# Two buffers of x and of the outputs, a new order of steps, and products of q on GpSimd in a linear-attention and rational-feed-forward kernel

## The chip, the cores and the metric

The kernel runs on one core of a Trainium2 chip. The time is that of one execution on the device in microseconds; lower is better. The core has five engines that run their own instruction lists in order and wait for each other by semaphores: TensorE (PE; PEld is its loading of weights), VectorE (DVE), ScalarE (ACT), GpSimd (POOL) and SyncE (SP), which here only issues DMAs. Sixteen DMA engines serve the queues of SP, GpSimd and ACT.

## The reference

```python
# attention: q, k, v, f_logit are (4, 8, 768, 48)
f = 1.0 / (1.0 + np.exp(-f_logit))
for t in range(S):
    state = f[:, :, t, :, None] * state + np.einsum('bhd,bhe->bhde', k[:, :, t], v[:, :, t])
    y[:, :, t] = np.einsum('bhd,bhde->bhe', q[:, :, t], state)
# x: y as (3072, 384); w_in (384, 2048), w_out (2048, 384)
h = x @ w_in
h2 = h * h
h3 = h2 * h
P = a[0] + a[1] * h + a[2] * h2 + a[3] * h3
Q = 1.0 + np.abs(b[0]) * np.abs(h) + np.abs(b[1]) * h2
g = P / (Q + 1e-06)
out = g @ w_out
```

## The kernel before, in words

The work is cut into 12 units of 256 positions. Unit n belongs to batch n % 4 and to the third n // 4 of its sequence, so unit n needs the state that unit n-4 left. A unit has two parts of 128 positions, j = 0 and 1.

Nothing is scheduled by a planner at build time. A long text, `ORDER`, lists every step by hand-readable name, and the kernel emits the steps in that order; each engine runs its own steps in the order of the text. `@i` names the PSUM slot (four of them, of two banks each). `!m` marks a step, and `^m` makes another begin only behind the marked one. The text calls the second pair a tie: products on GpSimd begin behind a chosen VectorE step, `wi` (loads of w_in) behind the landing of unit 1's k (`^w`).

The steps of a unit, with the engine and the line of the helper:

- `ld n f|k|q|v` loads (L205): f, k, q on SP's queue, v on GpSimd's. f, k, q and v have three buffers each. A load in two pieces is written `ld 0 k 0 2; ld 0 k 2 4`.
- `ef`, `ls` (ACT, L279, L284): exp and log of the gate, as log f; `cs` (PE, L294, L299): its running sum by triangular matrices.
- `A n x` (ACT, L307): exp of the running sum, for q (x = 0) and k (x = 1). There is one buffer for each x, so the next unit's `A` waits until the product has read it. `ae` (ACT, L438) does the same for a whole part.
- `xa n x` (L312): the product of q or k with `A`, on VectorE, or on GpSimd where a `p` stands behind it.
- `T`, `Te`: transposes of both products on PE (L326), and their copy out of PSUM (L333), on ACT where an `s` stands behind it and else on VectorE.
- `sc`, `mk` (PE L347, DVE L355): scores and their mask. `vm` (L362) copies pieces of v. `yi`, `yb` (PE, L367): y from the state and from the scores. `ic`, `si`, `st` (PE L413, L422, DVE L442): the next state.
- `ye` (ACT L430 or DVE L432): y scaled into x in bf16.
- `h` (PE, L451): a group of four blocks of x times w_in, twelve matmuls; `hy` (ACT, L468) copies them out; 16 blocks to a unit.
- `sq`, `ab`, `p1`, `p2`, `pm`, `gm` (DVE, L472 to L534): squares, absolute values, the numerator and the quotient.
- `zd` and `ta` (L498, L526): additions made by adding DMAs from GpSimd's queue; `zv` and `tv` (DVE, L494, L530) are the same additions on VectorE, and `u` with `ln` (PE L484, ACT L489) is a third way for the first one.
- `lz`, `ex` (ACT, L502, L507): the reciprocal of Q as the exp of minus its log.
- `o` (PE, L543): g times w_out; `oe` (L550): its copy; `so` (L559): two stores on SP's queue.

Before, x has four buffers, and the outputs one, `osb`; the last three units write their outputs into the buffers of f, which are free by then.

## Time and profile before

| | |
|---|---|
| median of 3 runs | 223.18 us (222.46 to 224.02) |
| the profiled execution's own time | 221.77 us |
| its span, first to last instruction | 220.1 us |
| ACT busy | 196.8 us (89%) |
| DVE busy | 196.3 us (89%) |
| PE busy | 193.1 us (88%) |
| POOL busy | 82.3 us (37%) |
| data moved | 44.23 MB, mean 201 GB/s |
| granted TensorE clock | 0.987 |

A busy share is an average over the whole span. Which engine sets the end has to be read stage by stage, from the windows and the chain of waits. Instructions of ACT and DVE overlap a little with the next of the same engine, so a duration is somewhat longer than the distance from one start to the next. Each row of a timeline gives start and duration in us, engine, line, operation, output and input tiles, and in brackets the idle time before it and what ended it.

### The profile page before, as it was taken

Reading aid. Unit: us, or ns where it says so; the run is one execution under the profiler, and the core shown is the slowest. Engines: PE = TensorE matmul, PEld = TensorE weight load, DVE = VectorE, ACT = ScalarE, POOL = GpSimd, SP = SyncE. Lnnn points to the kernel's source line nnn. Section 1 sums busy time; section 2 is a strip of 40 time slices with the busy share of each in tenths; the row PEclk is TensorE's granted clock in tenths of the full one; section 3 lists DMA queues with packets and bytes.
Section 4 is the critical chain, followed back from the end, with each engine's and each line's share of the span. In section 5 each row is a group of like instructions: output and inputs, shape, how many; then the busy total and the mean of one; then the engine's idle time right before and its main releaser. Section 6 shows DMA issues by size and latency. Waiting matters only on the chain.

```text
span 220.1 us, 7002 instructions
## 1 busy us (share of the span) xinstructions
PE 193.1 (88%) x3112; PEld 140.1 (64%) x3112; DVE 196.3 (89%) x186; ACT 196.8 (89%) x186; POOL 82.3 (37%) x95
## 2 busy tenths in 40 slices
PE   0569679588998998999999999899899999999991
PEld 0447468467685776686686677676686776865650
DVE  1668858999999999998999999999998999999761
ACT  4734389999999999999999999999999999999970
POOL 7039050293506552415325455335438303331100
PEclk9996999999999999999999999999999999999997
DMA  5999999999999999999799999999799998999964
GB/s 132 196 267 236 215 242 203 260 234 212 192 200 199 158 209 199 254 225 225 172 171 217 240 216 252 200 189 180 138 191 224 194 199 181 191 172 180 189 152 134
DMA packets 62110, 44.23 MB, mean 201 GB/s; under 512 B 51456, under 2 KB 56576, under 8 KB 62080
## 3 DMA queue, kind: packets, MB, share of 16 engines
q0 software_dynamic: 20816, 24.91, 68.6%
q1 hardware_dynamic: 40976, 18.88, 35.6%
q8 instruction: 24, 0.39, 0.7%
q10 hardware_dynamic: 288, 0.00, 0.1%
q14 instruction: 6, 0.05, 0.1%
HBM read 25.17 MB, written 4.72 MB: 136 GB/s over the span
## 4 chain that ended last, share of the span: by engine, by line
ACT 64%; DMA 12%; issue 10%; SPq 7%; PE 3%; DVE 2%; ACTq 0%; DVEq 0%
ACT hy L468 16%; ACT lq L502 14%; ACT qi L507 14%; DMA f<-in_f_logit_dram 7%; SPq L205 6%; ACT T L333 5%; ACT A L307 5%; DMA out_dram<-osb 5%; PE op L543 3%; ACT x L430 2%; ACT lsp L284 2%; ACT f L279 2%; ACT osb L550 2%; ACT lq L489 2%; DVE g L534 1%
## 5 line engine op out<-in xcount | busy, mean ns | idle before, releaser
L451 PE MATMUL hp<-x,w_in_sb 128*128 128x256 bf16 x576 | 67.9, 272 | 4.9 <-DMA w_in_sb<-in_moe_w_in_dram 2.7
L543 PE MATMUL op<-w_out_sb,g 128*128 128x384 bf16 x384 | 69.0, 326 | 0.8 <-ACT hy L468 0.7
L451 PEld LDWEIGHTS <-w_in_sb 128*128 128x128 bf16 x576 | 55.7, 98 | 14.3 <-issue 6.4
L468 ACT CAST hy<-hp 128x1024 bf16<-128x1024 f32 x48 | 50.2, 1130 | 1.5 <-PE hp L451 1.5
L543 PEld LDWEIGHTS <-g 128*128 128x128 bf16 x384 | 35.9, 98 | 23.5 <-DVE g L534 1.1
L507 ACT ACTIVATE qi<-lq 128x4096 bf16<-128x4096 f32 (+2 forms) x17 | 45.5, 2695 | 0.1
L502 ACT ACTIVATE lq<-z 128x2048 f32<-128x2048 bf16 x22 | 43.8, 2011 | 0.4 <-DMA z<-h 0.3
L498 POOL DMA_DIRECT2D z<-h x18 | 17.8, 1045 | 45.8 <-DVE z L476 29.3
L472 DVE TENSOR_TENSOR h<-hy 128x4096 bf16<-128x4096 bf16 (+1 forms) x14 | 27.7, 1977 | 3.1 <-ACT hy L468 3.1
L355 DVE TENSOR_TENSOR scm<-sc,mask 128x1024 bf16<-128x1024 f32 x24 | 28.4, 1215 | 1.5 <-PE sc L347 1.4
L534 DVE TENSOR_TENSOR g<-g,qi 128x4096 bf16<-128x4096 bf16 (+2 forms) x17 | 28.1, 1659 | 1.6 <-ACT qi L507 1.4
L526 POOL DMA_DIRECT2D g<-hy x19 | 18.4, 1053 | 29.5 <-DVE hy L517 6.8
L522 DVE TENSOR_TENSOR g<-g,h 128x4096 bf16<-128x4096 bf16 (+1 forms) x13 | 27.5, 2118 | 0.0
L312 POOL TENSOR_TENSOR qkp<-k,A 128x768 bf16<-128x768 f32 x10 | 18.9, 1888 | 20.5 <-DMA q<-in_q_dram 9.6
L307 ACT ACTIVATE A<-cs 128x768 f32<-128x768 f32 (+1 forms) x26 | 21.2, 869 | 3.3 <-DVE qkp L312 2.7
L205 POOL DMA_DIRECT2D v<-in_v_dram x12 | 13.0, 1085 | 18.7 <-PE y L367 10.3
L279 ACT ACTIVATE f<-f 128x768 f32<-128x768 f32 (+1 forms) x13 | 11.3, 890 | 7.2 <-DMA f<-in_f_logit_dram 7.2
L294 PE MATMUL cs<-lsp,Ui 128*128 128x384 bf16 (+1 forms) x39 | 11.1, 344 | 7.6 <-ACT lsp L284 7.0
L326 PE MATMUL tp<-ident,qkp 128*128 128x128 bf16 x192 | 14.5, 231 | 3.7 <-ACT hy L468 0.9
L312 DVE TENSOR_TENSOR qkp<-q,A 128x768 bf16<-128x768 f32 (+1 forms) x13 | 11.6, 888 | 6.0 <-ACT A L307 5.5
L333 ACT COPY T<-tp 128x2048 bf16<-128x2048 bf16 x8 | 16.2, 2028 | 0.0
L512 DVE TENSOR_SCALAR g<-hy,a_sb 128x4096 bf16<-128x4096 bf16 x12 | 16.1, 1339 | 0.0
(70 smaller groups left out, 249.6 us busy)
## 6 DMA issues: line engine op xcount, KB each, us to landing
g<-hy POOLq DMA_DIRECT2D x19, 512.0 KB, 8.0
z<-h POOLq DMA_DIRECT2D x18, 512.0 KB, 7.0
f<-in_f_logit_dram SPq DMA_DIRECT2D x11, 384.0 KB, 8.8
k<-in_k_dram SPq DMA_DIRECT2D x11, 384.0 KB, 9.1
q<-in_q_dram SPq DMA_DIRECT2D x11, 384.0 KB, 9.3
out_dram<-osb SPq DMA_DIRECT2D x18, 192.0 KB, 5.8
v<-in_v_dram POOLq DMA_DIRECT2D x12, 192.0 KB, 8.3
w_in_sb<-in_moe_w_in_dram POOLq DMA_DIRECT2D x8, 192.0 KB, 7.8
```

The lines of the kernel that those rows point to most:

```text
L307: nc.scalar.activation(t, src, AF.Exp, scale=1.0 if x else -1.0)
L312: i = (nc.gpsimd if eng == "p" else nc.vector).tensor_mul(s["qk"][:, x, :, hh, 0:D], s["qk"[x]][:, hh].rearrange("p h i d -> p i h d"), s[ ...
L333: return (nc.scalar.copy if "s" in args else nc.vector.tensor_copy)(s["T"][:, :, :, a0:a1].rearrange("p x i a t -> p (x i) (a t)"), s["tp" ...
L355: return nc.vector.tensor_mul(t, s["sc", g].rearrange("s r a i t -> s (r a) (i t)"), mb)
L451: nc.tensor.matmul(t[:, m - m0, :].rearrange("f (j t) -> f j t", j=UB), w_in_sb[:, kk, m * P:(m + 1) * P], s["x"][:, :, kk, :], start=(kk ...
L468: nc.scalar.copy(fl(big(s, "hy"), m0, m1), fl(s["hp", m0], 0, m1 - m0))
L472: return nc.vector.tensor_mul(fl(big(s, "h2"), m0, m1), fl(big(s, "hy"), m0, m1), fl(big(s, "hy"), m0, m1))
L502: nc.scalar.activation(fl(lq, m0, m1), fl(big(s, "z"), m0, m1), AF.Ln, scale=regs[2], bias=1.0 + 1e-6)
L507: nc.scalar.activation(fl(qi, m0, m1), fl(lq, m0, m1), AF.Exp, scale=-1.0)
L522: return nc.vector.tensor_mul(fl(big(s, "g"), m0, m1), fl(big(s, "g"), m0, m1), fl(big(s, "h2"), m0, m1))
L534: return nc.vector.tensor_mul(fl(big(s, "g"), m0, m1), fl(big(s, "g"), m0, m1), fl(qi, m0, m1))
L543: nc.tensor.matmul(s["op", g][:, j, 0:DM], big(s, "g")[:, m, C * j:C * j + C], w_out_sb[:, m, :], start=(s["on", j] == 1), stop=(s["on", j ...
```

## The change

Three things change. `x` goes from four buffers to two, and `osb` from one to two, which rotate over all units; outputs no longer use the buffers of f. The order text is new from the first line to the last. In it, some products are placed otherwise: of q (x = 0) on GpSimd in units 1, 6, 7, 8, 9 and 11, of k (x = 1) on GpSimd in units 2, 3, 4, 5, 6, 8 and 10 (before: k in units 1 and 3 to 11, q in none). 13 products stand on GpSimd instead of 10. In units 6 and 8 both are there, the second without a tie of its own. `ye` is on VectorE in unit 1 instead of units 0 and 10. `vm` of units 0 and 1 moves to VectorE. Adding DMAs: 16 `zd` and 21 `ta` (before 18 and 19); on VectorE 6 `zv` and 3 `tv` (before 4 and 5). The two `u` groups that were of unit 1 are of unit 0. The copy of unit 10's outputs is on VectorE instead of unit 9's.

```diff
 ORDER = """
-ab_ b a; ld 0 f 0 2; cz 3; cu 1; cz 2; cz 0; ld 0 f 2 4; ld 0 q 0 2; cu 0; ld 0 k 0 2; ci; ld 1 f; ld 0 v
-ld 1 k !w; ld 1 v; ef 0 0 2; ab_ a a; ls 0 0 2; ld 0 k 2 4; ef 0 2 4; cs 0 0 2 @0; ld 0 q 2 4; A 0 1 0 2
-A 0 0 0 2; ls 0 2 4; ld 1 q; xa 0 0 0 2; cs 0 2 4 @1; cz 1; cm; ef 1; xa 0 1 0 2; ae 0 0 2; ls 1; fa; T 0 0 2 @2
...
+ld 0 f 0 2; cz 1; ci; ld 0 f 2 4; cz 3; cu 1; cz 2; cz 0; ld 1 f; ld 0 k 0 2; cu 0; ld 0 v; ld 0 k 2 4; cm
+ld 0 q 0 2; ld 1 v; ef 0 0 2; ab_ b a; ld 0 q 2 4; ef 0 2 4; ld 1 k !w; ls 0 0 2; ls 0 2 4; cs 0 0 2 @0
+si 0 0 @1; A 0 0 0 2; cs 0 2 4 @2; ld 1 q; ae 0 0 2; ab_ a a; ef 1; fa; ls 1; ae 0 2 4; A 0 0 2 4; cs 1 @3
+A 0 1 0 2; ld 2 f; A 0 1 2 4; xa 0 1 0 2; xa 0 1 2 4; A 1 1; ic 0; xa 0 0 2 4; xa 0 0 0 2; ld 3 f; si 1 0 @0
+A 1 0; T 0 0 2 @2; ae 1; ld 2 q; Te 0 0 2; wi 1 0 8 ^w; st 0 0; wi 3 0 8 ^w; sc 0 0 @3; xa 1 1; T 0 2 4 @2
+wi 0 0 8 ^w; ld 2 k; wi 2 0 8 ^w; Te 0 2 4 !x1; ic 1; mk 0 0; ef 2; sc 0 1 @2; xa 1 0 0 4 p ^x1; si 0 1; ls 2
+mk 0 1; cs 2 @3; wi 0 8 16 ^w; vm 0 v; st 0 1; wi 3 8 16 ^w; T 1 @2; st 1 0; A 2 1; wi 1 8 16 ^w; fb; ef 3
+wi 2 8 16 ^w; yi 0 1 @1; yb 0 2 4; Te 1; ae 2; fr; yb 0 0 2; ls 3; si 1 1; st 1 1; A 2 0; vm 1 v; cs 3 @2
+ld 6 f; ld 3 k; ye 0 s; xa 2 0 !x2; sc 1 0 @0; ld 4 f; sc 1 1 @3; ae 3; mk 1 0; A 3 0; h 0 0 4 @1; mk 1 1
+xa 2 1 0 4 p ^x2; h 0 4 8 @0; hy 0 0 4; ld 2 v; T 2 @3; hy 0 4 8; A 3 1; yi 1 1 @1; sq 0 0 8; yb 1 0 2; ld 3 q
+Te 2 s; h 0 12 16 @0; ab 0 0 8; ld 5 f; zv 0 0 8; yb 1 2 4; hy 0 12 16; sc 2 0 @2; ye 1 v !x3; sc 2 1 @3
+lz 0 0 8; h 0 8 12 @0; mk 2 0; xa 3 1 0 4 p ^x3; ld 4 k; h 1 4 8 @1; mk 2 1; hy 0 8 12; ld 5 q; ef 6; ld 3 v
...
+p2 2 0 16; lz 2 8 16; o 1 1 8 12 @3; ld 9 f; o 1 1 4 8; sq 3 0 16 !x6; ta 2 0 8; sc 5 1 @2
+oe 0 0 2 s; ld 7 k; si 5 0 @1; o 1 1 12 16; ta 2 8 16; lz 2 0 8; o 1 0 0 4; ld 7 q; o 1 1 0 4; vm 5; mk 5 1
+xa 6 0 0 4 p ^x6; ic 5; ef 7; sc 5 0 @0; st 5 0; o 1 0 12 16; ex 2 0 16; mk 5 0; si 5 1; xa 6 1 0 4 p; o 1 0 4 8
...
+o 9 0 12 16; lz 10 8 16; p1 11 0 16; so 8 0 2; u 11 0 4 @0; so 7 0 2; u 11 4 8 @3; gm 10 0 8; ln 11 0 4
+o 9 0 0 4; p2 11 0 16; ex 10 8 16; o 10 1 4 8 @1; o 10 0 4 8; pm 11 8 16; o 10 1 0 4; ln 11 4 8; o 9 1 8 12
+gm 10 8 16; o 10 0 0 4; ta 11 8 16; ex 11 0 4; o 9 0 8 12; pm 11 0 8; ex 11 4 8; o 10 1 8 12; oe 9 0 2 s
+o 10 1 12 16; tv 11 0 8; o 10 0 12 16; lz 11 8 16; so 9 0 2; o 10 0 8 12; gm 11 0 4; gm 11 4 8; o 11 1 0 4 @0
+oe 10 0 2 v; ex 11 12 16; o 11 1 4 8; o 11 0 0 4 @3; ex 11 8 12; so 10 0 2; gm 11 12 16; o 11 0 4 8; gm 11 8 12
+o 11 0 12 16; o 11 0 8 12; o 11 1 12 16; oe 11 0 1 s; o 11 1 8 12; so 11 0 1; oe 11 1 2 v; so 11 1 2
 """
...
-    rings("x", 4, [UB, KD, C], BF16)
+    rings("x", 2, [UB, KD, C], BF16)
     rings("ae", 2, [HP, UB], F32)
-    rings("osb", 1, [UB, DM], F32)
+    rings("osb", 2, [UB, DM], F32)
...
     def oe(n, j0, j1, eng="v"):
         s = unit(n)
-        s["osb"] = ring["osb"][0] if n < UNITS - 3 else (
-            ring["f"][n % 3].rearrange("p h i d -> p (h i d)").rearrange("p (j d) -> p j d", j=UB))
+        s["osb"] = ring["osb"][n % len(ring["osb"])]
```

## The prediction, made before the changed kernel ran

> **What bounds the kernel now.** I read the busy table first, then three stretches, then ScalarE's own list, then the chain of waits, and last the DMA queues of the head.

> ```profile
> span 220.1 us, 7002 instructions
> ...
> PE 193.1 (88%) x3112; PEld 140.1 (64%) x3112; DVE 196.3 (89%) x186; ACT 196.8 (89%) x186; POOL 82.3 (37%) x95
> ```

> Three engines near 89% say little alone. The windows (PE, PEld, DVE, ACT, POOL busy) say more:

> ```profile
> 31.00:204.00 173.00, 164.32 (x2662) 120.32 (x2661) 170.14 (x133) 172.59 (x153) 69.28 (x68) 1.00 1.08 203
> 204.00:220.10 16.10, 11.43 (x69) 6.22 (x67) 7.94 (x10) 9.07 (x9) 0.86 (x1) 0.93 0.66 157
> 0.00:31.00 31.00, 17.39 (x385) 13.59 (x386) 18.25 (x45) 15.14 (x26) 12.19 (x27) 0.94 1.11 215
> ```

> From 31 to 204 us ScalarE (ACT) is busy 172.6 of 173 us and VectorE (DVE) 170.1. So the time is a head until ACT is full, ACT's work, and a tail. ACT's timeline shows where the head ends (start, duration, idle before it in brackets):

> ```profile
> 25.01 0.79 ACT L307 ACTIVATE A<-cs 128x768 f32<-128x768 f32 x1
> 27.28 1.01 ACT L468 CAST hy<-hp 128x1024 bf16<-128x1024 f32 x1 [1.48 <-PE hp L451]
> 28.19 0.82 ACT L307 ACTIVATE A<-cs 128x768 f32<-128x768 f32 x1
> 28.89 1.02 ACT L468 CAST hy<-hp 128x1024 bf16<-128x1024 f32 x1
> 29.79 0.21 ACT L438 ACTIVATE ae<-cs 128x8 f32<-128x8 f32 x1
> 30.75 0.85 ACT L279 ACTIVATE f<-f 128x768 f32<-128x768 f32 x1 [0.75 <-DMA f<-in_f_logit_dram]
> ```

> Neighbours overlap, so I cost an ACT step by the distance between starts: `hy` 0.90, `A`, `x` and output copies 0.69, `f` and `ls` 0.73, `lz` 1.81, `Te` 1.75, `ex` of 16 blocks 3.51. "Lost time" of a step is its start less the sum of these costs ahead of it. In the kernel before it is 4.5 at the first step (f of unit 0 lands), 17.2 at the first `hy` (27.28 less 10.1 of work), 18.1 behind `ef 3`, 18.25 at 63 us, 20.3 at `ex 10 8 16` (203.6 less 183.3). So all but 2 us are lost by 31 us, and ACT's order in the head decides.

> **Head: the loads.** The DMA view in two stretches, 11 to 15 and 20 to 28 us:

> ```profile
> DMA packets 3015, 1.11 MB, mean 278 GB/s; under 512 B 3015, under 2 KB 3015, under 8 KB 3015
> ...
> q1 hardware_dynamic: 2908, 1.09, 118.7%
> ```
> ```profile
> DMA packets 1794, 1.72 MB, mean 215 GB/s; under 512 B 1154, under 2 KB 1154, under 8 KB 1793
> ...
> q0 software_dynamic: 745, 1.31, 87.3%
> q1 hardware_dynamic: 1048, 0.40, 24.8%
> ```

> q1 is SP's queue (f, k, q), q0 GpSimd's (w_in, v, the adding DMAs). Alone SP moves 270 KB/us; beside w_in only 0.40 MB in 8 us, 50 KB/us, while w_in gets 163 KB/us, 1.16 us a piece of 192 KB.

> So I count SP's loads by place; landing times are those of the trace's DMA records. Before, the k load of unit 2 was ninth in full-size loads (3456 KB, landed 23.2), f of unit 3 tenth (3840 KB, landed 30.72, because w_in went first). The new order of SP's queue is f0, f1, k0, q0, k1, q1, f2, f3, q2, k2: q2 is now ninth, k2 tenth. What is wanted with k2:

> - w_in starts behind k1, as before. k1 was at 1536 KB (12.83); now it is at 1920 KB, where q0 landed at 14.15. So w_in's first issue goes from 13.11 to 14.4. Its four first pieces are now issued in a row; data moved 2.75 us behind the issue, so from 17.2 to 21.9 (4 x 1.16). SP by then has 3.23 MB through: f3 lands near 20.
> - The other four pieces stand behind unit 1's product of q on GpSimd, tied to the second `Te` of unit 0. From q0's last half (14.15 less 1.3, as it is now seventh: 12.8): products 1.2, transposes 0.7, `Te` 0.7, state 0.5, product of unit 1 0.9, `Te` 0.7 give 17.6; the product takes 1.83, so 19.5, and the data moves from about 22.4 to 27.1. In the gap of 0.5 us SP gets 130 KB, then 50 KB/us. q2 (3456 KB) lands near 26, k2 (3840 KB) is through at 28 and lands at 30.4, as f3 did with the same bytes ahead (30.72).
> - k2 then goes through GpSimd (1.83), unit 2's transposes (1.05, the row of T 2 in the timeline of PE), and only then `Te 2 s` can run: 33.5. In ACT's new list `Te 2 s` has only 14.8 us of work ahead of it (before: 21.6, at 39.8), so the lost time there is 18.7. The next `hy` waits for a matmul group queued behind those transposes (0.7 for y, 1.5 for h, less 1.75 of `Te`): 0.4 more. Lost 19.1 against 18.2: **+0.9**. `A 3 0` ahead of `hy 0 0 4` waits for unit 2's product on q2, to 27.4; that is lost 15.8 and hidden by the later wait. The new list has 2.2 us more work ahead of the first `hy` (12.3 against 10.1), which would have been a gain.

> Ends: k2 half a microsecond early and no stall behind `Te`, 0; k2 at 31.5 and transposes at 1.9 us, as T 1 took, +2.8. I take 0.9.

> **Work.** ACT gets `ye 0` and `ye 10` and gives `ye 1`: one step, 0.69. Up to the end of `ex 10 8 16` it also has one more output copy (0.68) and one `ln` less (0.90): **+0.5**; the rest comes behind it. DVE loses three full products (2.6), one x (0.9), and two adds `tv` (2.3), gains two `zv` (2.3) and two `vm` (0.6, bounded by GpSimd's 0.41 and a product's 0.95): 2.8 us less with the small splits. It is not the later engine, so I count 0. Its mean product is 0.95, GpSimd's 1.83; three more are 5.5 us of GpSimd, which is 37% busy. Adding DMAs: `zd` 18 to 16, `ta` 19 to 21, so their number is the same. PE has the same matmuls.

> **Buffers.** With two of x, `ye n` waits for the last `h` of unit n-2. In ACT's work between the two places the closest pair is unit 2, 10.5 us apart: 0. With two of outputs, the copy of unit n waits for the store of n-2. Early stores were never on ACT's waits with one buffer. The last three units lose their own places in the f buffers. There the store of unit 7 is issued behind that of 8, in ACT's work 6 us ahead of the copy of unit 9; the same store before took 200.1 to 206.7, and unit 9's store (3.4 us to land before) must be down before `oe 11`. **+0.3**, between 0 and 2.

> The middle's other 2.0 us of waits I leave as they are, and PE's last stretch too: before, from `ex 10 8 16` (205.5) three DVE steps lead to the last unit's 32 matmuls (5.5 us), then copy and store, 14.6 in all:

> ```profile
> 205.54 1.23 DVE g L534
> 206.77 1.15 DVE g L522
> 207.94 1.24 DVE g L530
> ...
> 210.01 5.51 PE op L543 x32
> 215.54 0.56 DVE f L550
> ```

> The same chain follows in the new order.

> **Sum.** 220.1 + 0.9 + 0.5 + 0.3 = 221.8 span; with the 1.67 us around it (221.77 less 220.1), 223.5 against the profiled 221.77. The runs' median is 223.18, so on that scale **224.9**, 0.8% slower. A measurement here tells about 1%, 2.2 us.

> **Rivals.**
> 1. *k2 comes early, not slower.* If GpSimd's product of unit 1 begins 1.8 us later than my 17.6, w_in's second half begins behind q2 and k2: 610 KB at 265 are 2.3 us from 21.9, so k2 lands near 26 and `Te 2` has lost 14.5. Then w_in's second half decides: down near 31, `h` 1.5, so `hy 0 12 16` at 32.5 with 16.5 of work ahead: lost 16.0, 2.2 less than before. 223.18 - 2.2 + 0.8 = **221.8**. For it: ACT does more work early, and the tie chain is long. Against: the same bytes are due by 30.5 in both. It decides from 19.4 on.
> 2. *A load in the middle is late.* k of unit 11 is issued behind a store, with 10 us of ACT's work to its product; k and q of unit 11 took 13.4 and 13.7 us beside the adding DMAs, which leave SP almost nothing. 3.4 us of wait ahead of unit 11's transposes: **228.3**. Against: there is a gap in the adding DMAs just then.
> 3. *GpSimd's products hold up DVE.* The copy `vm` on GpSimd has a median of 406 ns and once took 2750 beside DVE work. In units 6 and 8 both products are on GpSimd, 3.66 us, under masks and states of 3.2: 0.5 each, hidden by DVE's 5.7 free us. If the second one waits for k and falls on the two-input steps, 1.83 each, of which half reaches ACT: **226.7**. [...]
> 4. *Output buffers at the end* at their upper end, 2 us: **226.6**.

> **Chances.** Forecast 0.45 (0.30 within 1%, 0.15 above, as its own ends are 223.7 to 227), rival 1 0.25 (half below 1%, as head waits could fall further), rival 2 0.15, rival 3 0.07, rival 4 0.08. So faster 0.13, within 1% 0.42, slower 0.45. Range 221.5 to 228.3, from rival 1 to rival 2; the forecast's own is 223.7 to 227.

> **What would show it.** Right: `Te 2` on ACT starts near 33.5 with a wait ahead of it and at `A 3 1`; k2 lands at 30 to 31; ACT full from there; DVE 2 to 4 us less busy. Wrong: k2 lands before 28; ACT's idle time in the first 35 us falls by over 1 us; or gaps of over 1 us on ACT between 60 and 200 us, above all at units 6 and 11.

## The result, and the profile after

The changed kernel took **230.14 us** (median of four runs, 227.96 to 230.45) where the kernel before took 223.6 in the same set. The ratio is **1.0282, with a 95% interval of 1.0234 to 1.033**: 2.8% slower. The forecast was 224.9, in a range of 221.5 to 228.3. So the sign was right, and the size was not. The profiled execution took 229.95 us, and its span grew from 220.1 to 228.2.

The busy table of the page after, to be read against the two lines shown of before:

```profile
span 228.2 us, 7016 instructions
...
PE 198.9 (87%) x3112; PEld 143.6 (63%) x3112; DVE 197.0 (86%) x186; ACT 198.4 (87%) x187; POOL 93.6 (41%) x96
```

TensorE has the same 3112 matmuls and is busy 5.8 us longer. So many of its matmuls ran slower. VectorE is not 2 to 4 us less busy, as I had said, but 0.7 more.

ScalarE's timeline after, where the head ends (start, duration, idle before it):

```profile
32.45 0.81 ACT L307 ACTIVATE A<-cs 128x768 f32<-128x768 f32 x1 [2.95 <-POOL qkp L312]
34.85 1.86 ACT L333 COPY T<-tp 128x2048 bf16<-128x2048 bf16 x1 [1.59 <-PE y L367]
37.23 1.01 ACT L468 CAST hy<-hp 128x1024 bf16<-128x1024 f32 x1 [0.51 <-PE hp L451]
```

These are `A 3 1`, `Te 2 s` and `hy 0 12 16`. The waits stand where the prediction put them, but `Te 2` starts at 34.85 and not at 33.5. And there is a new gap far behind, in unit 8's `ye`:

```profile
144.92 0.81 ACT L430 ACTIVATE x<-y 128x768 bf16<-128x768 f32 x1 [2.50 <-PE y L367]
```

I take lost time (start less the work ahead, by the prediction's costs) at three places: at `hy 3 8 12`, where the head and its after-effects are over (63 us before, 73 after); at the start of `ex 10 8 16`; and the rest of the span from there.

| | before | after | difference | forecast |
|---|---|---|---|---|
| lost by `hy 3 8 12` (head) | 18.25 | 22.14 | +3.9 | +0.9 |
| lost from there to `ex 10 8 16` (middle) | 2.02 | 5.51 | +3.5 | 0 |
| ScalarE's work up to there | 183.32 | 183.79 | +0.5 | +0.5 |
| from there to the end (tail) | 16.51 | 16.76 | +0.2 | +0.3 |
| span | 220.1 | 228.2 | +8.1 | +1.7 |

Of the head's 3.9, 2.7 are lost by `hy 0 12 16` (37.23, above). Another 1.1 come at 60 to 62 us, behind a stretch at half clock (0.50 from 56.22 to 59.63):

```profile
56.22:59.63 3.41, 3.41 (x18) 2.45 (x17) 3.41 (x4) 3.41 (x2) 3.18 (x3) 0.50 1.06 208
```

Of the middle's 5.5, 2.8 come at `ye 8 s` (the gap above) and 1.5 at `hy 8 4 8`, 7 us later. TensorE's timeline there:

```profile
140.36 0.33 PE L367 MATMUL y<-scm,vmp 64*32 64x128 bf16 x16
140.47 0.33 PE L367 MATMUL y<-scm,v 64*32 64x128 bf16 x12
144.07 0.29 PE L367 MATMUL y<-scm,vmp 64*32 64x128 bf16 x8 [3.27 <-issue]
144.19 0.23 PE L367 MATMUL y<-scm,v 64*32 64x128 bf16 x4
144.35 0.52 PE L367 MATMUL y<-T,state 128*32 128x128 bf16 x24
144.80 1.77 PE L326 MATMUL tp<-ident,qkp 128*128 128x128 bf16 x16
```

TensorE stands still for 3.5 us from start to start, in the middle of one step, and the reason given is "issue": it waits for nothing that the profile shows. The transposes behind it take 1.77 us, where those of unit 2 before took 1.06. The windows there (column behind POOL: granted clock) show why:

```profile
140.00:144.00 4.00, 0.80 (x53) 0.59 (x52) 3.97 (x2) 2.42 (x3) 0.00 (x0) 1.00 1.06 218
144.00:146.00 2.00, 1.93 (x49) 1.72 (x50) 0.00 (x0) 1.08 (x2) 0.00 (x0) 0.74 1.04 178
146.00:148.00 2.00, 2.00 (x19) 1.31 (x17) 1.39 (x2) 2.00 (x1) 0.00 (x0) 0.50 0.50 134
148.00:150.00 2.00, 2.00 (x18) 1.57 (x16) 2.00 (x2) 2.00 (x3) 0.38 (x1) 0.90 0.00 0
```

The DMA view has one more queue, of instructions (q8). It carries 24 pieces of 16 KB in the whole span, and one of them moves just here, 141.81 to 142.74 (window 141.5 to 143):

```profile
DMA packets 135, 0.30 MB, mean 202 GB/s; under 512 B 36, under 2 KB 82, under 8 KB 134
...
q0 software_dynamic: 66, 0.21, 78.6%
q1 hardware_dynamic: 68, 0.07, 17.7%
q8 instruction: 1, 0.02, 3.9%
```

TensorE has 6245 recorded instructions, 6224 of them matmuls and weight loads; over 24 pieces these are 260 to a piece, and the stops found below stand whole multiples of 256 apart. So the first theory, the **code theory**: the pieces are TensorE's own instructions, this one came late, and TensorE ran on at a low clock.

Its rivals: the **products theory** (GpSimd's products hold up VectorE, the prediction's rival 3), the **buffers theory** (two of x, two of outputs), and for the head the question whether the order itself loses 3.9 us.

### The profile page after: what moved, and what is told of

It is laid out like the page before. It is cut to its first block, busy times and chain, and to the rows that moved or that the text cites. A ratio compares the mean times of both kernels' runs of the same rounds, so it can differ in the third digit from the quotient of the medians.

```text
span 228.2 us, 7016 instructions
## 1 busy us (share of the span) xinstructions
PE 198.9 (87%) x3112; PEld 143.6 (63%) x3112; DVE 197.0 (86%) x186; ACT 198.4 (87%) x187; POOL 93.6 (41%) x96
## 3 DMA queue, kind: packets, MB, share of 16 engines
q1 hardware_dynamic: 40976, 18.88, 34.3%
## 4 chain that ended last, share of the span: by engine, by line
ACT 36%; DVE 19%; issue 14%; DMA 11%; PE 10%; SPq 6%; POOL 2%; ACTq 0%; POOLq 0%; DVEq 0%
ACT qi L507 9%; ACT hy L468 8%; ACT lq L502 7%; DMA k<-in_k_dram 6%; SPq L205 6%; DMA z<-h 5%; DVE scm L355 4%; DVE g L522 3%; ACT T L333 3%; PE hp L451 3%; DVE hy L517 2%; DVE g L512 2%; PE op L543 2%; ACT A L307 2%; ACT osb L549 2%
## 5 line engine op out<-in xcount | busy, mean ns | idle before, releaser
L451 PE MATMUL hp<-x,w_in_sb 128*128 128x256 bf16 x576 | 70.6, 277 | 3.7 <-ACT hy L468 1.3
L543 PE MATMUL op<-w_out_sb,g 128*128 128x384 bf16 x384 | 68.8, 327 | 0.7 <-ACT hy L468 0.3
L451 PEld LDWEIGHTS <-w_in_sb 128*128 128x128 bf16 x576 | 56.5, 99 | 14.7 <-issue 5.6
L468 ACT CAST hy<-hp 128x1024 bf16<-128x1024 f32 x48 | 49.5, 1077 | 2.8 <-PE hp L451 2.6
L543 PEld LDWEIGHTS <-g 128*128 128x128 bf16 x384 | 36.1, 98 | 23.7 <-DVE g L534 1.2
L526 POOL DMA_DIRECT2D g<-hy x21 | 22.3, 1161 | 47.3 <-PE hp L451 15.9
L355 DVE TENSOR_TENSOR scm<-sc,mask 128x1024 bf16<-128x1024 f32 x24 | 28.5, 1216 | 2.4 <-PE sc L347 2.2
L534 DVE TENSOR_TENSOR g<-g,qi 128x4096 bf16<-128x4096 bf16 (+2 forms) x18 | 28.2, 1577 | 1.5 <-ACT qi L507 1.4
L498 POOL DMA_DIRECT2D z<-h x16 | 18.5, 1172 | 25.1 <-issue 8.8
L307 ACT ACTIVATE A<-cs 128x768 f32<-128x768 f32 (+1 forms) x26 | 19.8, 803 | 9.4 <-DVE qkp L312 4.1
L522 DVE TENSOR_TENSOR g<-g,h 128x4096 bf16<-128x4096 bf16 (+1 forms) x13 | 27.7, 2133 | 0.0
L312 POOL TENSOR_TENSOR qkp<-k,A 128x768 bf16<-128x768 f32 x7 | 13.2, 1888 | 22.4 <-DMA k<-in_k_dram 8.5
L326 PE MATMUL tp<-ident,qkp 128*128 128x128 bf16 x192 | 16.3, 249 | 5.6 <-POOL qkp L312 4.0
L326 PEld LDWEIGHTS <-qkp 128*128 128x128 bf16 x192 | 14.0, 112 | 7.5 <-POOL qkp L312 4.3
L294 PE MATMUL cs<-lsp,Ui 128*128 128x384 bf16 (+1 forms) x39 | 12.2, 376 | 6.9 <-ACT lsp L284 6.7
L476 DVE TENSOR_SCALAR z<-hy 128x4096 uint16<-128x4096 uint16 (+1 forms) x14 | 16.8, 1202 | 0.6 <-ACT hy L468 0.6
L512 DVE TENSOR_SCALAR g<-hy,a_sb 128x4096 bf16<-128x4096 bf16 x12 | 16.7, 1393 | 0.5 <-ACT hy L468 0.5
L333 ACT COPY T<-tp 128x2048 bf16<-128x2048 bf16 x8 | 15.4, 1930 | 1.6 <-PE y L367 1.6
L517 DVE TENSOR_SCALAR hy<-hy,a_sb 128x4096 bf16<-128x4096 bf16 x12 | 16.5, 1375 | 0.0
```

Of the source, the lines that this page charges most:

```text
L307: nc.scalar.activation(t, src, AF.Exp, scale=1.0 if x else -1.0)
L326: nc.tensor.transpose(t[:, x, i, p, :], s["qk"][:, x, i, 2 * p:2 * p + 2, :].rearrange("t h d -> t (h d)"), ident)
L355: return nc.vector.tensor_mul(t, s["sc", g].rearrange("s r a i t -> s (r a) (i t)"), mb)
L451: nc.tensor.matmul(t[:, m - m0, :].rearrange("f (j t) -> f j t", j=UB), w_in_sb[:, kk, m * P:(m + 1) * P], s["x"][:, :, kk, :], start=(kk ...
L468: nc.scalar.copy(fl(big(s, "hy"), m0, m1), fl(s["hp", m0], 0, m1 - m0))
L522: return nc.vector.tensor_mul(fl(big(s, "g"), m0, m1), fl(big(s, "g"), m0, m1), fl(big(s, "h2"), m0, m1))
```

## The experiments

### The same kernel again, and 60 or 30 matmuls of no use

> The changed kernel once more, unaltered. Code theory (TensorE stops at 140.6 us in the middle of unit 8's y because the next 16 KB of its instructions arrive late, 489 of its instructions behind the piece before instead of about 256): the place is set by the instruction stream, so the stop is again within a few instructions of the 4288th, 1 to 4 us long. Chance theory (a late transfer that this execution alone had): no stop there, time near 226. Head theory: unit 2's copy of the transposes (Te 2) has lost 20 us again (34 to 35.5 us), since unit 2's k lands last at 29.5 to 30.7.

230.64 us (one run). The stop is back at the same matmul, 3.75 us long.

```
+ ... cz 0; wm 0 60 @3; ld 1 f; ...          (or: wm 0 30 @3)
  def wm(n, count, sl):
-     nc.tensor.matmul(t[:, i % 2, 0:HP * W], ident, state(unit(3), 0), ...)
+     nc.tensor.matmul(t[0:32, i % 2, 0:32], ident[:, 0:32], state0[:, 0, 0:32], ...)
```

> The changed kernel with 60 tiny TensorE matmuls (with their weight loads 120 instructions) in the first 5 us, where TensorE is idle. Only the borders of its 16 KB pieces of code move, by 120 of the program's own instructions. Code theory: no stop inside y of unit 8 at the old place; the fetch is asked for some 3 us earlier, ahead of the adding DMAs of unit 6, and the 4.3 us that ScalarE loses at ye 8 and hy 8 fall to under 1: 225.5 to 227 against the changed 230. If the fetch is as late as before, the stop moves to 120 instructions earlier in the program. Order theory (y of unit 8 waits for something the new order makes late: v, mask, GpSimd's copy): the stop stays in y of unit 8, time as the changed kernel within 1.

**225.49 us, ratio 1.0043 (0.999 to 1.0096).** The stop in unit 8's y is gone; one of 1.75 us stands at 161 us. The ratio fell from 1.0282 to 1.0043 by an edit that only adds instructions, done before TensorE has anything else to do. Of the 4.5 us that the span lost in the profile, the middle has 3.6. The head has 1.1, the loss at 60 to 62 us, which this run doesn't have.

> As the run before with 30 tiny matmuls, 60 instructions. Code theory: if a stop comes, it is 60 of the program's own instructions earlier than in the changed kernel (in h of unit 7 or the o group ahead of y of unit 8), not inside y of unit 8. Order theory: inside y of unit 8.

225.6 us (one run). The stop moved to steps 60 of the kernel's own recorded instructions earlier, and was 1.94 us. Another of 2.9 us appeared at 90 us, on another border. So the stops did not get shorter in sum, and the middle still lost 3.9 us. The time is low because the head lost only 19.23, and the clock fell behind neither stop.

### The same 60 in the kernel before, and 128 in the changed one

> The kernel before with the same 60 tiny matmuls in TensorE's queue in its first 5 us, where TensorE has nothing else to do (they add work of no use, into PSUM that is overwritten later). If the stops of TensorE at fixed places of its instruction stream are the cause of the loss, this kernel too can change by a few microseconds in either direction, since its places move, although no work on the later path is changed: I expect a time between 221 and 228, and that lost time of ScalarE appears or vanishes at other steps than in the kernel before. If the 60 matmuls help in themselves (a warmer TensorE at the start, say), this kernel should be about as much faster than the kernel before as the same edit made the changed kernel: 4 us, 219.5.

227.46 us, ratio **1.0113 (1.005 to 1.0175)**: the edit that made the changed kernel 2% faster makes the kernel before 1.1% slower. In the profile the span is 4.3 us longer, 3.2 of it in the middle and 1.0 in the head. A stop appears in unit 10's first group of `h`, which `hy 10 0 4` waits for (lost time there +2.79):

```profile
172.21 0.27 PE L451 MATMUL hp<-x,w_in_sb 128*128 128x256 bf16 x1
175.22 2.47 PE L451 MATMUL hp<-x,w_in_sb 128*128 128x256 bf16 x11 [2.73 <-issue]
```

> The changed kernel with 128 tiny matmuls in TensorE's queue at the start instead of 60. Each is two instructions of TensorE, so this shifts its stream by 256, which is the distance found between the places of the stops and the size of one 16 KB piece. If only the place within a piece counts, the stop is back at the same instructions of the kernel, in unit 8's y, 3 to 3.8 us long, and the time is 230 to 231. If the 60 matmuls helped by anything else (a TensorE awake at the start, loads that come earlier), this kernel is fast too: 225 to 226.

227.47 us (one run). 128 pairs shift the stream by 256, and the stop is back at the very same matmuls:

```profile
138.77 0.33 PE L367 MATMUL y<-scm,v 64*32 64x128 bf16 x12
141.97 0.34 PE L367 MATMUL y<-scm,vmp 64*32 64x128 bf16 x8 [2.88 <-issue]
```

The place is as expected and the rival is out. The time is under what I expected, 230 to 231: the head lost 1.9 us less in this run (20.24 by `hy 3 8 12`), and the stop was 3.1 us.

### Why the piece is late

I put the DMA records of the pieces beside TensorE's records. In all 18 traces, with either order, every stop on "issue" of over 0.75 us between 60 and 200 us (27 of them) stands within 3 recorded instructions behind 190 + 256 n. Nearly all pieces move after TensorE has crossed the border ahead of them. A few are up to 1.8 us early, and the last piece of a run mostly up to 2.2; why is not known. Times in us, stops over 1 us and one without:

| kernel, piece | border ahead crossed | piece moved | at the piece's border | instructions of the piece before lasted | stop |
|---|---|---|---|---|---|
| after, 16 | 136.49 | 141.81 to 142.74 | 140.58 | 4.09 | 3.49 |
| after, 12 | 103.50 | 108.33 to 109.28 | 109.66 | 6.17 | 1.15 |
| after, 11 | 93.22 | 97.22 to 98.18 | 103.52 | 10.30 | none |
| after again, 16 | 137.06 | 142.59 to 143.52 | 141.14 | 4.08 | 3.75 |
| 128 in front, 17 | 134.80 | 139.56 to 140.53 | 138.88 | 4.08 | 3.09 |
| 60 in front, 19 | 155.06 | 158.65 to 159.62 | 159.24 | 4.18 | 1.75 |
| before, 18 | 150.27 | 152.97 to 153.94 | 154.35 | 4.08 | 0.82 |
| before with 60, 21 | 168.91 | 172.78 to 173.67 | 172.21 | 3.29 | 3.00 |

In each row with a stop TensorE runs on 1.2 to 1.6 us after the piece has landed (144.07 less 142.74 is 1.33). So in these rows a stop comes where 256 instructions are run in less time than the piece's lag, its 0.9 us of transfer and these 1.3 us. 256 instructions mostly last 5 to 13 us. Where scores, states and y of a unit stand close together, 64-column matmuls, they last 4.1. Before has such places too (piece 18), with a lag of 2.7 instead of 5.3, and stands still there for 0.8 us:

```profile
154.34 0.22 PE L367 MATMUL y<-scm,vmp 64*32 64x128 bf16 x3
155.16 0.28 PE L367 MATMUL y<-scm,vmp 64*32 64x128 bf16 x5 [0.60 <-issue]
```

Over nine runs (180 pieces from the fourth on), the lag has a median of 1.3 us where the adding DMAs' queue was under 20% busy around the border (37 pieces), and 3.2 us elsewhere. Two runs try this:

```
- ... zd 6 0 8 ... zd 6 8 16 ...
+ ... zv 6 0 8 ... zv 6 8 16 ...      (VectorE instead of adding DMAs)
```

> The changed kernel with the two adding DMAs of unit 6's first addition (issued at 133.7 and 135.7 us, landing at 144.1 and 146.8) made on VectorE instead, 2.3 us more of its work. TensorE's instruction stream is the same. If those DMAs hold up the transfer of TensorE's next instructions, the stop at its 4286th recorded instruction falls from 3.5 us to under 1 us and the time is 226 to 229 (4.3 us less by the stop and the clock behind it, up to 2.3 more by VectorE). If the transfer is asked for late whatever else moves, the stop stays at the same instruction with 3 us or more, and the time is 230 to 232.5.

230.78 us (one run). Inconclusive: the piece moved at 140.55, 137 instructions ahead of need, and the stop in y is gone. But VectorE, now 2.3 us longer in that place, finished unit 8's state late, and TensorE waited for that in its place:

```profile
141.14 2.72 PE L451 MATMUL hp<-x,w_in_sb 128*128 128x256 bf16 x12 [1.66 <-DVE state L442]
```

In this run the granted clock is 0.50 from 140.01 to 146.84, so from the last part of that wait on:

```profile
141.00:143.00 2.00, 1.86 (x9) 1.28 (x9) 2.00 (x4) 0.53 (x1) 0.00 (x0) 0.50 0.48 127
143.00:146.00 3.00, 3.00 (x64) 1.82 (x63) 2.94 (x2) 1.76 (x2) 0.00 (x0) 0.50 0.00 1
```

A wait of 1.7 us on TensorE and the low clock around it cost ScalarE 4.3 (lost time +2.63 at `hy 7 8 12`, +1.65 at `ye 8 s`).

```
- p1 6 0 16; ld 11 q; zd 6 0 8; ...   ic 8; zd 6 8 16; lz 5 0 8; ...   xa 9 0 0 4 p ^x9; mk 8 1; ...   vm 9; pm 6 0 16;
+ p1 6 0 16; ld 11 q; ...             ic 8; lz 5 0 8; ...   xa 9 0 0 4 p ^x9; zd 6 0 8; mk 8 1; ...   vm 9; zd 6 8 16; pm 6 0 16;
```

> The changed kernel with the two adding DMAs of unit 6's first addition moved behind unit 9's product of q in GpSimd's queue, so that they start near 138.5 us and later instead of at 133.7 and 135.7. TensorE, VectorE and ScalarE have the same instructions in the same order. If a load of the DMA engines ahead of the late piece is what delays it, the piece moves before TensorE's 4160th recorded instruction, the stop in unit 8's y falls below 1 us, and the time is 226 to 227.5. If the piece is asked for late whatever else moves, it moves when TensorE stands at its 4286th instruction, the stop is 3 us or more, and the time 229.5 to 231.5.

**225.37 us, ratio 1.0118 (1.0018 to 1.0217).** Neither theory's numbers hold whole. The piece moved 137.63 to 139.19, a lag of 3.8 us instead of 5.3, and the stop was 2.73 us, so it was not gone:

```profile
137.82 0.33 PE L367 MATMUL y<-scm,v 64*32 64x128 bf16 x12
140.66 0.29 PE L367 MATMUL y<-scm,vmp 64*32 64x128 bf16 x8 [2.52 <-issue]
140.79 0.23 PE L367 MATMUL y<-scm,v 64*32 64x128 bf16 x4
140.94 0.52 PE L367 MATMUL y<-T,state 128*32 128x128 bf16 x24
141.39 1.07 PE L326 MATMUL tp<-ident,qkp 128*128 128x128 bf16 x16
```

But the transposes behind it took 1.07 us, at a granted clock of 1.00, and `hy 8 4 8` lost nothing. The head of this run lost 18.88, close to the forecast, though nothing in it was changed. So of the 5.0 us of span against the changed kernel, 3.3 are the head, which varies between runs, and 1.7 are the middle. The middle's gain is the edit's as far as one profile tells, and 1.5 of it is the clock, which did not fall.

### Both edits together

> Both edits that helped: the two adding DMAs of unit 6 later, and the 60 tiny matmuls at the start. If the stop at the border of a piece and the low clock behind a stop are what is left of the loss, no stop of over 1 us stands between 60 and 200 us, lost time of ScalarE between 63 us and the last exp is 2 us as in the kernel before, and with the head between its values so far (18.9 to 21) the time is 222.5 to 225, a ratio of 0.997 to 1.008. If the change costs something else that the stops have hidden so far, the ratio stays at 1.01 or more although no such stop is there.

**225.35 us, ratio 1.0073 (1.0037 to 1.0109).** No stop of over 1 us is left between 60 and 200 us. The middle loses 0.88, under the 2.02 of before. The head lost 21.37, the rest is as in the changed kernel. With the late code gone, the change is 0.7% slower (the kernel before keeps its own stop of 0.8 us). In the profiles the head loses 3.1 us more than before, work and tail 0.9, and the middle 1.1 less.

### The products and the buffers

In the changed kernel, q's products in units 6 to 9 and 11 went back to VectorE, and k's in 7, 9 and 11 to GpSimd, where they stood before:

```
- xa 7 0 0 4 p ^x7; ... xa 7 1;
+ xa 7 1 0 4 p ^x7; ... xa 7 0;       (likewise 9 and 11; in 6 and 8 one product back to VectorE)
```

> The changed kernel with the products of units 6, 7, 8, 9 and 11 placed as before the change (k on GpSimd, q on VectorE; GpSimd has 11 products instead of 13), all else and TensorE's instruction list unaltered. Code theory: TensorE's stop at its 4288th instruction stays, time within 1 us of the changed kernel's 230. Products theory (q on GpSimd, two in a row in units 6 and 8, make y of unit 8 late): 3 us or more faster, and no stop in y of unit 8.

229.77 us, ratio 1.0316 (1.0194 to 1.0439). The profiled execution took 232.85 us, 3 us above the median, so only the place of the stop is read from it: the same matmul. The products theory falls for these units. Unit 2's products stood as in the changed kernel.

In the kernel before:

```
- xa 7 1 0 4 p ^x7; ... xa 7 0;        xa 6 0; ... xa 8 0;
+ xa 7 0 0 4 p ^x7; ... xa 7 1;        xa 6 0 0 4 p; ... xa 8 0 0 4 p;     (9 as 7)
```

> The kernel before with only the products: q on GpSimd in units 6 to 9 (k too in units 6 and 8), where units 7 and 9 give k to VectorE. Own sum: VectorE has two products less (1.8 us), which is not the later engine; GpSimd's second products in units 6 and 8 have no tie and may fall on VectorE steps with two inputs: 0 to 2 us slower. Products theory: over 3 us slower.

227.6 us, ratio 1.0242 (1.0097 to 1.0387). This says little on the places. VectorE idled 2.87 us ahead of unit 7's product of k, to 107.36, though that k had landed at 92.83:

```profile
107.36 0.96 DVE L312 TENSOR_TENSOR qkp<-k,A 128x768 bf16<-128x768 f32 x1 [2.87 <-DMA k<-in_k_dram]
```

What landed at 107.24 was unit 10's k. The order text says why: k has three buffers, so units 7 and 10 share one, and here `ld 10 k` stands ahead of `xa 7 1`. By the text the product waits for unit 10's k and works on it in place of unit 7's. TensorE's clock behind that wait was 0.60 (108 to 112 us), and the middle lost 4.0 us more than before. The changed kernel has no such wait at unit 7.

```
- rings("x", 4, ...); rings("osb", 1, ...); s["osb"] = ring["osb"][0] if n < UNITS - 3 else (...)
+ rings("x", 2, ...); rings("osb", 2, ...); s["osb"] = ring["osb"][n % len(ring["osb"])]
```

> The kernel before with only the buffers changed: two of x, two of outputs that rotate over all units. My own sum: 0 to 0.3 us at the end, so within 0.5% of before. Buffers theory (the last stores hold up the copies, or x is too short): 1 us or more slower, with ScalarE's lost time rising behind oe 8.

225.28 us, ratio 1.0137 (0.9973 to 1.03): unclear. The span in its profile is 2.9 us longer. The head has 2.0 of it, with the clock at 0.50 from 26.2 to 29.6 and from 43.2 to 46.6. The tail has 0.8: in the order of before `oe 11` waits for a store, 2.46 us instead of 0.97 for TensorE:

```profile
217.20 0.48 ACT L549 COPY osb<-op 128x384 f32<-128x384 f32 x1 [2.46 <-DMA out_dram<-osb]
```

In the changed kernel that copy waits 1.64 us, for TensorE.

### The head

```
- ... hy 0 0 4; ld 2 v; T 2 @3; hy 0 4 8; A 3 1; ... Te 2 s; h 0 12 16 @0; ... hy 0 12 16; sc 2 0 @2; ... lz 0 0 8; h 0 8 12 @0; ...
+ ... hy 0 0 4; ld 2 v; hy 0 4 8; ... h 0 12 16 @0; ... hy 0 12 16; T 2 @3; A 3 1; lz 0 0 8; Te 2 s; sc 2 0 @2; ... h 0 8 12 @0; ...
```

> The changed kernel with unit 2's transposes on TensorE and A 3 1 and Te 2 on ScalarE moved behind the third h group of unit 0 and, for Te 2, behind lz 0 0 8. Head theory (the steps that want unit 2's k stand too early): lost time behind the head falls from 20.7 to 18 to 19, so 2 us less: 227.5 to 228.5 if the stop at unit 8 stays. Rival (the head is bound by the loads whatever stands there, and something else of the head waits as long): within 0.7 of the changed kernel.

234.72 us, ratio 1.0455 (1.0357 to 1.0554). A miss: `h 0 8 12` now stood behind the scores, these behind the later `Te 2`, and TensorE idled 4 us.

A better order has both last groups of unit 0 ahead of unit 2's transposes, and unit 2's product of q behind unit 1's masks:

```
+ ... mk 1 0; h 0 0 4 @1; mk 1 1; xa 2 0 !x2
+ ... hy 0 0 4; hy 0 4 8; ... h 0 12 16 @0; yb 1 2 4; h 0 8 12 @3; ... hy 0 12 16; hy 0 8 12; A 3 0; A 3 1
+ T 2 @3; Te 2 s; sc 2 0 @2; ...
```

> The changed kernel with its head reordered so that nothing of unit 0 stands behind unit 2's q and k: masks of unit 1 ahead of unit 2's product on VectorE; on ScalarE all four hy of unit 0 ahead of A 3 0, A 3 1 and Te 2; on TensorE the transposes of unit 2 behind both last h groups of unit 0, the fourth in another PSUM slot. Head theory: Te 2 near 35 us with 16.5 us of work ahead of it instead of 14.8: lost time behind the head 18.3 to 19, 2 us less, so 228 with the stop at unit 8 still there. Rival (the head is held by w_in's second half or by something that no step order moves): lost time stays above 20.

230.84 us, ratio 1.0378 (1.0247 to 1.051). Up to `Te 2` it lost 19.2, as expected. Then TensorE, after a wait of 2.1 us, ran 24 matmuls in 4.4 us at a clock of 0.50 to 0.84, and the loss was 21 again.

The same with the 60 matmuls at the start:

> The changed kernel with the reordered head of the last head run and the 60 tiny matmuls. The long stop in unit 8 should be gone as it was with the 60 matmuls alone (225.5), and the head should lose about the same as there (20.7 to 21), since the reordered head alone gained nothing by its end: 225 to 226.5. If the low clock behind the wait for unit 2's transposes is absent here, the head loses 19.2 and the time is 223.5 to 224.

226.08 us, ratio 1.0087 (1.0028 to 1.0145): no better than the 60 alone.

The changed head with the 60 matmuls, and unit 2's product of k on VectorE:

```
- xa 2 1 0 4 p ^x2; h 0 4 8 @0; ...
+ xa 2 1; h 0 4 8 @0; ...
```

> The changed kernel with the 60 tiny matmuls, and unit 2's product of k on VectorE instead of GpSimd. Theory of the head (GpSimd's product takes 2.3 us and holds up VectorE's two-input step beside it): the product is done 1.3 us earlier behind k2 (0.95 for 2.3), the absolute value beside it takes 0.7 again instead of 2.3, unit 2's transposes start near 31.1, and ScalarE has lost 19.2 to 19.6 at the first group behind Te 2 instead of 20.7: about 224.3, against 225.5 with the 60 matmuls alone. Rival (only the landing of k2 and the low clock of the transposes count): the transposes start earlier but the loss at that group stays above 20.3, and the time at 225.5 or, with 0.9 us more of VectorE, 226.

225.39 us, ratio 1.0033 (0.9984 to 1.0082), against 225.49 without it. The product took 0.96, the absolute value 0.69, the transposes 1.10, as the theory said. But q2 landed at 28.55 and k2 at 32.84 in this run, and the clock was 0.50 from 30.6 to 34.0 ahead of the transposes, so the gain is not to be seen. Not settled by it.

Eight profiles have the changed kernel's head as it is, or with only the matmuls of no use at the start (that of 232.85 us left out). By `hy 3 8 12` they lost 22.14, 22.37, 20.99, 19.23, 21.95, 20.24, 18.88 and, with both edits, 21.37 us. The first two hold the 1.1 us at 60 to 62 us. In the three best, unit 2's transposes took 1.07 us at a clock of 0.79 to 1.00 (windows of 2 us). In three others they took 1.5 to 1.9, at 0.50 to 0.70, and in the changed kernel's profile 1.89, at 0.58. Before, and after:

```profile
36.59 1.06 PE L326 MATMUL tp<-ident,qkp 128*128 128x128 bf16 x16
```
```profile
32.47 1.89 PE L326 MATMUL tp<-ident,qkp 128*128 128x128 bf16 x16 [4.03 <-POOL qkp L312]
```

In the run of both edits the clock fell only behind them (0.50 from 34 to 36), and the next twelve matmuls took 2.60 us instead of 1.49. TensorE waits up to 4 us for GpSimd's product of k just ahead. So a last run filled that wait:

```
- wm 0 60 @3 at the start
+ wm 0 46 @3 at the start; ... ld 2 v; wm 0 14 @3; T 2 @3; ...      (these 14 of full size)
```

> The last kernel (adding DMAs of unit 6 later, 60 matmuls of no use) with 14 of its 60 moved from the start into TensorE's queue ahead of unit 2's transposes, and made full size (128x384, some 0.16 us each, 2.3 us in all), where TensorE otherwise waits up to 4 us for the product of unit 2's k. If the low clock behind that wait makes the head's extra loss, the clock stays at 0.95 or more between 32 and 38 us, a group of twelve matmuls there takes 1.5 us instead of 2.6, ScalarE has lost 18.5 to 19.5 at 72 us instead of 21.4, and the time is 222.5 to 223.5, a ratio of 0.992 to 1.0. If these matmuls only fall on the path, or the clock drops all the same, the loss stays above 20.5 and the ratio at 1.004 to 1.012.

227.09 us, ratio 1.0154 (1.0092 to 1.0216). The clock stayed at 1.00 from 34 us on, with all groups at 1.48 there. But it had fallen before: q2 came late (27.7 us), TensorE waited 2.33 us for unit 1's masks, and from 30.03 to 33.44 the clock was 0.50. The group there took 2.72 us, and the added matmuls, begun at this clock, fell on the path:

```profile
30.01 2.72 PE L451 MATMUL hp<-x,w_in_sb 128*128 128x256 bf16 x12 [2.33 <-DVE scm L355]
32.52 2.90 PE L459 MATMUL wm<-state,ident 128*128 128x384 bf16 x14
35.48 1.05 PE L326 MATMUL tp<-ident,qkp 128*128 128x128 bf16 x16
```

So the run did not try what it was made for, a full clock between 32 and 38 us.

No version beat the kernel before.

## Why the prediction was wrong, point by point

**The step that failed** is the sentence "The middle's other 2.0 us of waits I leave as they are". The middle lost 3.5 us more. I had taken a new text of the order as the same matmuls, and so the same TensorE, without asking what else is in its stream. A new order also moves the borders of its pieces of code. One border fell behind 256 instructions that last 4.09 us, while the piece had a lag of 5.3 us beside the adding DMAs. That the stop of 3.5 us comes from the place of the border is shown by the shifts of 60, 30 and 128 and by the kernel before with 60. That the lag comes from the load on the DMA engines is made likely by the median over 180 pieces and by the run with the adds later (5.3 to 3.8), not shown.

**The clock** had no term at all. Behind the stop it cost 1.5 us more (`hy 8 4 8`). Its changes have a grid. In all 18 traces those between 5 and 210 us lie whole multiples of 3.41 us apart, and the low clock (0.50) lasts 3.41 us or a multiple: in the changed kernel from 32.33 to 35.74, from 56.22 to 59.63 and from 144.97 to 148.38. Windows of the changed kernel, cut there:

```profile
141.56:144.97 3.41, 0.90 (x39) 0.69 (x40) 2.41 (x2) 0.91 (x3) 0.00 (x0) 1.00 1.06 197
144.97:148.38 3.41, 3.41 (x31) 2.60 (x29) 1.77 (x2) 3.41 (x2) 0.00 (x0) 0.50 0.59 135
148.38:151.79 3.41, 3.41 (x29) 2.68 (x28) 3.41 (x3) 2.53 (x4) 1.91 (x3) 1.00 0.26 50
```

So the length of a stop alone does not decide. Stops of 3.49, 3.09 (128 in front) and 3.00 us (before with 60) left TensorE 0.90, 0.54 and 0.68 us of work in one such window, and 0.50 followed. Those of 2.94 (30 in front) and 2.73 (adds later) fell over two windows, with 1.8 to 2.4 us of work in each, and 1.00 followed: that is luck of place. Nor does the work in one window: with the adds on VectorE TensorE was busy 2.05 of 3.41 us (136.60 to 140.01), more than that 1.8, and 0.50 followed. What decides is open.

**The head** was the right mechanism with the wrong size: k2 landed at 29.96 (forecast 30.4), the waits were at `A 3 1` and `Te 2`, and ScalarE was full from `hy 0 12 16` to 60 us. The term +0.9 measured +2.7 there, and +3.9 by `hy 3 8 12` with the loss at 60 to 62 us, which no term had. Up to `Te 2` two things were added: GpSimd's product took 2.32 us instead of 1.83, and the transposes 1.89 instead of 1.05. My upper end, +2.8, had the transposes at 1.9, but at the price of a late k2, not of the clock. Over the eight profiles the head's term lies between +0.6 and +4.1.

**Work** (+0.5) held with +0.47. The tail came to +0.2 against +0.3 for the **buffers**, but no copy in it waits for a store, so the buffers are not what the 0.2 are. **VectorE** did lose the work that I counted, 13.6 to 10.6 us of products (L312). But the same number of steps of L476, L512 and L517 took 50.0 us instead of 47.1, so its busy time did not fall. 1.6 of these 3.0 us are one step of the head, `ab 0 0 8`.

**Rivals.** The first (k2 early) fell with k2 at 29.96. The second had nearly the size (228.3) and the right stage, with a wrong cause: no load was late in unit 11. The third (GpSimd's products hold up VectorE) has its mechanism in the traces. In four profiles the absolute value `ab 0 0 8` beside GpSimd's product took 2.29 or 2.30 us, where it took 0.68 or 0.69 without one. Before, and after with the square `sq 0 0 8` ahead of it:

```profile
31.09 0.69 DVE L476 TENSOR_SCALAR z<-hy 128x2048 uint16<-128x2048 uint16 x1
```
```profile
29.53 1.23 DVE L472 TENSOR_TENSOR h<-hy 128x2048 bf16<-128x2048 bf16 x1 [1.47 <-ACT hy L468]
30.67 2.29 DVE L476 TENSOR_SCALAR z<-hy 128x2048 uint16<-128x2048 uint16 x1
...
30.10 2.32 POOL L312 TENSOR_TENSOR qkp<-k,A 128x768 bf16<-128x768 f32 x1 [8.50 <-DMA k<-in_k_dram]
```

Each time the one that began later is the longer one. The square, with two inputs, ran when the product began, and the product took 2.32 instead of 1.81; `ab` began during the product and ended 0.5 us behind it. In the run with 60 in front it was the square that began second, by 0.01 us, and it took 2.87 instead of 1.23:

```profile
30.48 2.87 DVE L472 TENSOR_TENSOR h<-hy 128x2048 bf16<-128x2048 bf16 x1 [1.48 <-ACT hy L468]
...
30.47 1.80 POOL L312 TENSOR_TENSOR qkp<-k,A 128x768 bf16<-128x768 f32 x1 [8.94 <-DMA k<-in_k_dram]
```

So a step with two inputs (the square) and one with one (`ab`) were both held up. Masks were not: in the kernel before two of them took 2.35 us (99.94) beside a product of 1.83 (99.55), and the mean of a mask is 1.22 (L355). On the path the hold-up counted little in units 6 to 9 and 11: with the products back the time stayed. In the head it put 0.5 us on the product of unit 2's k, and `lz 0 0 8` did not wait for `ab`. The fourth (output buffers) fell for the changed order; in the order of before the new buffers do hold up `oe 11`.

With the stop gone, the ratio is 1.0073, and 224.9 to 223.18 was 1.0077. That is no merit of the sum: the head lost 2.2 us more than I said and the middle 1.1 less than before.

## What to carry to other kernels

A reordering of a long unrolled kernel moves the borders of the engine's own code: look in the DMA view for the instruction queue, mark where TensorE crosses 256 instructions fast (3.3 to 6.2 us at the stops in the table), and try there with less load on the DMA engines (it cut the lag from 5.3 to 3.8 us in the one run that tried). A wait of "issue" in the middle of one step, at the same place in each run, can be such a border; the landing of a piece 1.2 to 1.6 us ahead of its end, as in that table, tells it from a late load. A harmless shift of the stream, in both kernels, tells luck of place from the worth of the change before anything else is explained. And price a wait of TensorE at more than its length (here 4.3 us for 1.7), since the work behind it may run at half clock (0.50 from 140.01 to 146.84 there). When a step moves in such a text, look too at which load comes next into its buffer.
